# Two layers of Fourier mixing and an MLP on one core: who normalizes the first two pairs of tiles, in which order the first stage makes its parts, and where a weight copy stands

## Chip, cores and metric

The kernel runs on one core of a Trainium2 chip. The metric is the device time of one execution in microseconds (us), from the start of the program to its end; the time of a kernel is the median of its runs. The profile is taken in an execution of its own, and its span runs from the first to the last of the program's instructions.

## The reference, cut to what matters

```python
def layernorm(x, eps=1e-5):
    return (x - mean(x, -1)) / sqrt(var(x, -1) + eps)

def A(x, Cr, Ci, Dr, Di):            # x: 1 x 2048 x 576
    a = einsum("bsd,ed->bse", x, Dr)          # hidden DFT, 576 x 576
    b = einsum("bsd,ed->bse", x, Di)
    return einsum("ts,bse->bte", Cr, a) - einsum("ts,bse->bte", Ci, b)   # sequence DFT, 2048 x 2048

def B(x, w1, b1, w2, b2):            # 576 -> 4608 -> 576
    y = layernorm(x)
    h = gelu(einsum("bsd,df->bsf", y, w1) + b1)
    return einsum("bsf,fd->bsd", h, w2) + b2

for layer in range(2):
    x = x + A(layernorm(x), ...)
    x = x + B(layernorm(x), ...)
```

All data is fp32. The DFT matrices are inputs like any other.

## The kernel before, in words

**Products in three passes.** TensorE multiplies in the format fp32r. Each operand is kept as a high part (a copy rounded to fp32r, made by ScalarE) and a low part (the source less the high part, made by VectorE), and each product is three matmuls: high by high, high by low, low by high (`PASSES`). Large products are also cut into 2 x 2 blocks and done in seven block products instead of eight (`ORDER`, `RIGHT`, `LEFT`), which needs sums and differences of blocks as further operands.

**Stages.** For each of the two layers, a `Sequence` computes the sequence DFT of the normalized x (class `Sequence`, method `run`), leaving its two results per tile of 128 rows in DRAM (`uv_mid`). Then two halves follow, each with a `Hidden` stage (the hidden DFT from `uv_mid` with the matrix `dh`, and the second normalization) and the MLP. In layer 0 the sequence stage also splits w1 into its parts in the background and stores them in DRAM (`w1_parts`, generator `weights`, moved on by calls of `pump`); layer 1 finds them made.

**The first stage of `Sequence.run`.** The 16 tiles of x are handled as 8 pairs p, each 128 x 4 x 288. The first `PLAIN` = 2 rows of output tiles (t = 0, 1, called the plain tiles) are computed with the plain eight products while the pairs come in: `first_mms(p)` issues 48 matmuls of 288 columns, 24 for tile 0 in banks 4 to 7, then 24 for tile 1 in banks 0 to 3. They need, of pair p, the high and low part of the matrix block (`high_left` on ScalarE, `low_left` on VectorE, 128 x 1024) and of the normalized x (`high_z` on ScalarE, 128 x 864 and 128 x 288; `low_z` on VectorE, the same shapes). Beside that each pair gives four differences for the later block products: `right_sums` (one instruction of VectorE, two of GpSimd, into the single buffer `t`), `high_sums` (ScalarE) and `low_sums` (VectorE).

The order of this stage is written by hand in the generator `fill` (the loop `for p in range(NP)`, from L406): each engine gets its instructions in the order in which the calls stand there, and works through them strictly in that order. Before the change, one round p issues: statistics of pair p + 1 (`norm_stats`: bn_stats, bn_aggr and an addition on VectorE, then three small GpSimd instructions: power, product, negation), `high_sums(p - 1)`, `high_parts(p + 1)` (`high_left`, the normalization by ScalarE's activation with bias and scale at L244, `high_z`), `low_left(p)`, at p = 7 also `begin_steps`, then `low_sums(p - 1)`, `low_z(p)`, `right_sums(p)`. Layer 1 (`early` is true) has its first pairs prepared during the MLP before it and shares the rounds from p = 2 on.

**The steps.** After the pairs come 14 output tiles of seven block products each, 98 steps (t, i) in the order `ORDER`. A step is 24 matmuls of 288 columns (`mms`). `begin_steps` makes the first operands: two sums on VectorE (`sums(2)`, 128 x 1024 each) and the high part of step 0. In the loop of `run`, step n issues the low part of step n + 2 (`low`, VectorE; the profile shows all subtractions of the helper `sub` as L197, all additions of `add` as L194), the high part of step n + 3 (`high`, ScalarE, L631), its matmuls, then `post`, which takes the product out of its bank (ScalarE at L661 to L667, or VectorE), and two calls of `pump` unless i = 2. At i = 2 the block sums of the next tile are made (`sums`). The blocks of the sequence matrix (`in_cs`, 512 KB each) come through SyncE's queue into six buffers as they come free.

**The weights in the background.** Each two calls of `pump` make one part: a high part (ScalarE, L270 and L271), a low part (VectorE), and a store to `w1_parts` (SyncE, 320 KB). A part is made in one of three buffers in turn, so the high part of number m waits until the store of number m - 3 has landed.

**The queue.** All DMAs here are issued by SyncE (L191), in the order of the calls. `run` copies b1 into the core and `dh` (nine blocks of 288 KB) into the DRAM tensor `dh_mid`, just after the pairs; `dh_mid` is first read in the last output tile of the sequence stage (`Hidden.begin`).

**The plain tiles' results** are copied out of the banks by ScalarE (`first_post(t)`, four copies at L585) into one buffer that is allocated and freed at once, so the copies of tile 1 wait for the store of tile 0; both are issued after the last parts of the first stage. Step 0 of the steps uses bank 4, so it waits for the copies of tile 0.

## Time and profile before

| what | value |
|---|---|
| median of 3 runs | 2724.04 us (2722.75 to 2724.89) |
| the profiled execution | 2726.73 us |
| its span | 2724.9 us |
| TensorE clock granted, mean | 0.997 |
| TensorE busy | 98% |
| VectorE / ScalarE / GpSimd busy | 65% / 40% / 29% |
| DMA | 544.92 MB, mean 200 GB/s |

The profiled execution's span leaves 1.8 us around it to that execution's time. In timeline rows the columns are: start and duration in us, engine, line, operation, output<-input, shapes, count, and in brackets the idle time of the engine before it with what ended that wait. PE is TensorE, PEld its weight loads, DVE VectorE, ACT ScalarE, POOL GpSimd, SP SyncE; "q" stands for an engine's sequencer. A row can merge several instructions that follow each other closely, and a matmul's shown time includes its way through the array, so a busy PE is not a PE at its full rate: rates are read from counts. The window rows give, for a stretch, its length, the busy time and count of each engine, the granted clock, the share of the DMA engines and GB/s.

### The profile page before, as it was taken

The page shows a single profiled execution, that of the slowest core. Times are in us where ns is not written, and L with a number is a line of the kernel's source. Part 1 is how long each engine was busy: PE and PEld are TensorE (multiplying, and loading weights), DVE is VectorE, ACT ScalarE, POOL GpSimd, SP SyncE. Part 2 cuts the span into 40 slices and gives each one's busy share as a digit, 9 for nine tenths or more (in the row PEclk, how much of TensorE's full clock was granted, in tenths as well). Part 3 has the DMA queues.
Part 4 walks back from the last instruction along what each step waited for, and adds up shares of the span by engine and source line. Part 5 has one row for each costly group of instructions (what it writes and reads, how often), then busy time and mean ns, then how long its engine had stood idle before and what let it go on. Part 6 is the DMA issues. An engine that isn't in the chain of part 4 may idle for free.

```text
span 2724.9 us, 45273 instructions
## 1 busy us (share of the span) xinstructions
PE 2667.4 (98%) x17488; PEld 2498.5 (92%) x17488; DVE 1767.8 (65%) x2582; ACT 1098.2 (40%) x1838; POOL 797.0 (29%) x746
## 2 busy tenths in 40 slices
PE   7999999999999999999999999999999999999998
PEld 7999999888888988988899999998999999898988
DVE  8788876777776565556676666466555556555555
ACT  6555554544443343333344333344333324433331
POOL 5232234544434432222240000043222234322222
PEclk9999999999999999999999999999999999999999
DMA  5676775777777456666453333636666673666664
GB/s 202 235 242 233 239 274 173 254 259 281 270 265 278 154 176 194 193 207 211 152 202 141 122 120 119 201 118 200 194 192 196 190 274 104 211 193 194 193 194 149
DMA packets 209287, 544.92 MB, mean 200 GB/s; under 512 B 22048, under 2 KB 56864, under 8 KB 208928
## 3 DMA queue, kind: packets, MB, share of 16 engines
q1 hardware_dynamic: 209072, 542.02, 60.7%
q8 instruction: 139, 2.28, 0.3%
q14 instruction: 76, 0.62, 0.1%
HBM read 429.87 MB, written 114.72 MB: 200 GB/s over the span
## 4 chain that ended last, share of the span: by engine, by line
PE 82%; DVE 6%; issue 4%; DMA 3%; ACT 2%; POOL 2%; SPq 1%; DVEq 0%; ACTq 0%; POOLq 0%
PE bank L204 80%; DVE R L197 3%; DVE A L197 1%; PE bank L836 1%; DVE A L194 1%; DMA w_parts<-R 1%; POOL A L197 1%; DMA A<-in_w 1%; ACT R L631 1%; SPq L191 1%; DVE moments L234 0%; DMA A<-in_c 0%; ACT A L244 0%; POOL R L197 0%; DMA R<-w_parts 0%
## 5 line engine op out<-in xcount | busy, mean ns | idle before, releaser
L204 PE MATMUL bank<-R 128*128 128x288 f32 (+2 forms) x16972 | 2618.6, 315 | 47.0 <-DVE A L194 15.0
L204 PEld LDWEIGHTS bank<-R 128*128 128x128 f32 x16972 | 2444.0, 189 | 213.3 <-DVE A L194 30.0
L194 DVE TENSOR_TENSOR A<-bank,A 128x576 f32<-128x576 f32 (+3 forms) x808 | 567.6, 710 | 542.6 <-PE bank L204 469.1
L197 POOL TENSOR_TENSOR R<-A,R 128x512 fp32r<-128x512 f32 x288 | 382.7, 1341 | 915.7 <-ACT R L1205 889.3
L197 DVE TENSOR_TENSOR R<-A,R 128x1024 fp32r<-128x1024 f32 (+8 forms) x521 | 486.5, 955 | 72.3 <-ACT R L631 35.4
L194 POOL TENSOR_TENSOR A<-A 128x576 f32<-128x576 f32 (+2 forms) x102 | 133.0, 1308 | 557.3 <-ACT A L669 369.4
L1144 ACT ACTIVATE bank<-bank,b1t 128x512 f32<-128x512 f32 (+1 forms) x224 | 144.7, 646 | 370.5 <-DVE bank L194 253.9
L1205 ACT ACTIVATE R<-A 128x512 fp32r<-128x512 f32 x288 | 175.8, 628 | 269.8 <-DVE A L197 114.5
L197 POOL TENSOR_TENSOR A<-A 128x384 f32<-128x384 f32 (+2 forms) x154 | 196.2, 1276 | 271.3 <-DVE R L197 104.0
L194 DVE TENSOR_TENSOR bank<-bank,A 128x512 f32<-128x512 f32 (+1 forms) x228 | 152.5, 671 | 153.5 <-PE bank L204 152.7
L197 DVE TENSOR_TENSOR R<-bank,R 128x512 fp32r<-128x512 f32 x336 | 209.8, 639 | 59.2 <-ACT R L200 49.3
L631 ACT ACTIVATE R<-A 128x1024 fp32r<-128x1024 f32 x196 | 204.4, 1053 | 92.8 <-DVE A L197 70.4
L197 DVE TENSOR_TENSOR A<-A 128x1024 f32<-128x1024 f32 (+3 forms) x132 | 141.0, 1073 | 6.1 <-ACT A L244 2.1
L1171 ACT ACTIVATE A<-bank 128x512 f32<-128x512 f32 (+1 forms) x76 | 43.7, 575 | 240.0 <-PE bank L204 234.8
L1205 ACT ACTIVATE R<-bank 128x512 fp32r<-128x512 f32 x216 | 121.1, 594 | 34.2 <-PE bank L204 34.2
L270 ACT ACTIVATE R<-A 128x256 fp32r<-128x256 f32 x126 | 52.0, 412 | 118.2 <-DMA w_parts<-R 72.7
L197 DVE TENSOR_TENSOR A<-bank,A 128x512 f32<-128x512 f32 x144 | 98.0, 680 | 0.0
L200 ACT ACTIVATE R<-bank 128x512 fp32r<-128x512 f32 (+1 forms) x112 | 50.0, 492 | 88.0 <-PE bank L836 81.9
L244 ACT ACTIVATE A<-A,moments 128x576 f32<-128x576 f32 x64 | 53.7, 862 | 53.1 <-POOL moments L227 28.2
L1144 ACT ACTIVATE A<-bank,b1t 128x512 f32<-128x512 f32 (+1 forms) x76 | 50.6, 665 | 53.8 <-DVE bank L194 53.7
L671 DVE SCALAR_TENSOR_TENSOR A<-A 128x288 f32<-128x288 f32 x28 | 16.0, 572 | 79.4 <-POOL A L194 79.4
L271 ACT ACTIVATE R<-A,power,middle 128x128 fp32r<-128x128 f32 x126 | 60.7, 482 | 0.0
(58 smaller groups left out, 609.2 us busy)
## 6 DMA issues: line engine op xcount, KB each, us to landing
R<-w_parts SPq DMA_DIRECT2D x504, 320.0 KB, 3.4
R<-w_parts SPq DMA_DIRECT2D x189, 576.0 KB, 3.7
A<-in_cs SPq DMA_DIRECT2D x112, 512.0 KB, 4.2
w_parts<-R SPq DMA_DIRECT2D x126, 320.0 KB, 5.1
w_parts<-R SPq DMA_DIRECT2D x63, 576.0 KB, 5.9
uv_mid<-A SPq DMA_DIRECT2D x32, 576.0 KB, 2.8
A<-in_w SPq DMA_DIRECT2D x72, 192.0 KB, 5.2
R<-dh_parts SPq DMA_DIRECT2D x23, 576.0 KB, 10.3
```

The costliest lines, as they stand in the source:

```text
L191: nc.sync.dma_start(dst, src)
L194: engine.tensor_tensor(dst, a, b, op=op)
L197: engine.tensor_tensor(dst, a, b, op=OP.subtract)
L200: nc.scalar.activation(hi, src, AF.Copy)
L204: nc.tensor.matmul(o, a, b, start=start, stop=stop, skip_group_check=True)
L244: nc.scalar.activation(dst, src, AF.Identity, bias=mv[:, 4:5], scale=mv[:, 3:4])
L270: nc.scalar.activation(t[:, 1:4:2], src[:, 0:3:2], AF.Copy)
L271: nc.scalar.activation(t[:, 2], src[:, 1], AF.Identity, bias=power[:, 2:3], scale=middle)
L631: nc.scalar.activation(self.cells[t, i](2, NP, P)[:, 0], self.source(t, i), AF.Copy)
L1144: nc.scalar.activation(dst, src, AF.Gelu_apprx_tanh, bias=bias(f))
L1171: nc.scalar.activation(up, o, AF.Copy)
L1205: nc.scalar.activation(H[q, k](2, TC)[:, 0], src, AF.Copy)
```

## The change

1. **Normalization of pairs 0 and 1 of layer 0** moves from ScalarE to VectorE: two `tensor_scalar` instructions a pair (128 x 576, subtract the mean, multiply by the power), in place. GpSimd's product and negation for these two pairs go.
2. **A new prelude**: VectorE clears `middle`, ScalarE writes `power` from it (its first activation), and TensorE transposes the identity `WARM` = 56 times into an unused corner of bank 3.
3. **Order in `fill`**: in layer 0 `low_left` and `low_z` of pairs 0 and 1 come first in their rounds; from p = 2 on (both layers) `low_z(p)` comes ahead of `low_sums(p - 1)`, and `right_sums(p)` behind it. `begin_steps` moves from the middle of round 7 to behind the loop.
4. **Plain tiles**: `first_post(0)` is issued right behind the matmuls of the last pair, ahead of `begin_steps` and the last sums, and writes into one of the x buffers; tile 1 gets a buffer of its own.
5. **The copies of b1 and dh** leave their place behind the pairs; they are issued in step n = 7, `dh` as one DMA instead of nine.

```diff
+WARM = 56
...
-    def stats_of_pair(src):
+    def stats_of_pair(src, plain=False):
...
         nc.gpsimd.tensor_tensor(mv[:, :, 3], mv[:, :, 2], power[:, 0:2], op=OP.pow)
+        if plain:
+            return mv
         nc.gpsimd.tensor_tensor(mv[:, :, 4], mv[:, :, 0], mv[:, :, 3], op=OP.mult)
...
+                if p < 2 and not self.early:
+                    self.low_left(p)
+                    self.low_z(p)
+                    yield
                 if p + 1 < NP:
                     self.norm_stats(p + 1)
+                if p == 0 and not self.early:
+                    self.right_sums(0)
+                    self.load_some()
                 if p and (p != 1 or not self.early):
                     self.high_sums(p - 1)
...
                 yield
-                if p > 1 or not self.early:
+                if p > 1:
                     self.low_left(p)
                 if p == 3:
                     self.begin_loads()
-                if p == NP - 1:
-                    self.begin_steps()
+                if p > 1:
+                    yield
+                    self.low_z(p)
                 if p and (p not in (1, 3) or not self.early):
                     self.low_sums(p - 1)
-                if p > 1 or not self.early:
+                if p > 1 or p and not self.early:
+                    self.right_sums(p)
                     yield
-                    self.low_parts(p)
-                    yield
+            self.begin_steps()
             self.high_sums(NP - 1)
             self.low(*self.steps[0])
             self.high(*self.steps[1])
...
         def normalize(self, p):
             for h in range(2):
                 at = slice(2 * h, 2 * h + 2)
+                if p < 2 and not self.early:
+                    v, mv = self.x[p][:, at], self.mv[p][:, h]
+                    nc.vector.tensor_scalar(v, v, mv[:, 0:1], mv[:, 3:4], op0=OP.subtract, op1=OP.mult)
+                    continue
                 normalize(self.x[p][:, at], self.x[p][:, at], self.mv[p][:, h])
...
-        def low_parts(self, p):
-            self.low_z(p)
-            self.right_sums(p)
-            if p == 0:
-                self.load_some()
...
+            outs = [next(b for b in self.xs if b.at >= UV_AT + 4 * D)]
+            self.xs.remove(outs[0])
+            self.first_post(0, outs[0])
             for _ in self.pieces:
                 pass
             hidden.reserve()
-            if not self.early:
-                dma(b1t, b1)
-                for k in range(KH):
-                    dma(dhd[k], dh[k])
             steps = self.steps
             self.low(*steps[1])
             self.high(*steps[2])
-            for t in range(PLAIN):
-                self.first_post(t)
+            for t in range(1, PLAIN):
+                outs.append(A.alloc(2 * D))
+                self.first_post(t, outs[t])
...
                 self.post(t, i)
                 if t == NT - 1:
                     hidden.begin(self, ORDER.index(i))
+                if n == 7 and not self.early:
+                    dma(b1t, b1)
+                    dma(dhd, dh)
                 if i != 2:
                     pump()
                     pump()
...
+    nc.vector.memset(middle, 0.0)
+    nc.scalar.activation(power, middle.to_broadcast([P, 4]), AF.Copy)
     make_identity(nc, ident)
+    for n in range(WARM):
+        nc.tensor.transpose(bank[:, 3, 3 * P:], ident, ident)
```

More of the change, by code (lines that the diff above doesn't have):

```diff
@@ L503, in norm_stats @@
             if p not in self.mv:
-                self.mv[p] = stats_of_pair(self.x[p])
+                self.mv[p] = stats_of_pair(self.x[p], p < 2 and not self.early)
         def normalize(self, p):
@@ L578, in first_mms, with first_post @@
             clock[0] += 1
-        def first_post(self, t):
-            out = A.alloc(2 * D)
+        def first_post(self, t, out):
             uv = out(2, 2, DH)
@@ L587, in first_post @@
             dma(uvd[t], out(2 * D))
-            out.free()
         def load_block(self, t, k, block):
@@ L694, in run @@
             self.high(*steps[2])
-            for t in range(PLAIN):
-                self.first_post(t)
+            for t in range(1, PLAIN):
+                outs.append(A.alloc(2 * D))
+                self.first_post(t, outs[t])
+            for out in outs:
+                clock[0] += 1
+                out.free()
             for n, (t, i) in enumerate(steps):
```

## The prediction

> **What bounds the kernel now.** First the page, for the whole.
>
> ```profile
> span 2724.9 us, 45273 instructions
> PE 2667.4 (98%) x17488; PEld 2498.5 (92%) x17488; DVE 1767.8 (65%) x2582; ACT 1098.2 (40%) x1838; POOL 797.0 (29%) x746
> ```
>
> TensorE is the bound nearly everywhere, so an edit is worth what it takes from, or adds to, TensorE's stops and slow stretches. The change touches the two sequence stages alone; there I read the timeline from 0 to 135 us (layer 0) and from 1340 to 1445 us (layer 1), TensorE's rows first, then whoever releases them.
>
> ```profile
> 5.73 0.72 POOL L238 TENSOR_TENSOR moments<-moments,power 128x2 f32<-128x2 f32 x1 [4.18 <-DVE moments L237]
> 7.68 1.28 ACT L513 ACT_TABLE_LOAD   x1 [7.68 <-DMA A<-in_c]
> 9.94 1.61 ACT L244 ACTIVATE A<-A,moments 128x576 f32<-128x576 f32 x2
> 11.58 0.92 ACT L525 ACTIVATE R<-A 128x864 fp32r<-128x864 f32 x1
> 12.53 1.43 DVE L197 TENSOR_TENSOR R<-A,R 128x864 fp32r<-128x864 f32 x2 [1.02 <-ACT R L525]
> 12.55 0.61 PE L204 MATMUL bank<-R 128*128 128x288 f32 x1 [12.55 <-ACT R L525]
> 13.88 0.75 DVE L197 TENSOR_TENSOR A<-A 128x576 f32<-128x576 f32 x1
> 14.55 1.53 DVE L234 BATCH_NORM_STATS2 moments<-A 128x6 f32<-128x288 f32 x4
> 16.46 3.92 DVE L197 TENSOR_TENSOR R<-A,R 128x1024 fp32r<-128x1024 f32 x4
> 22.90 3.94 DVE L197 TENSOR_TENSOR R<-A,R 128x1024 fp32r<-128x1024 f32 x4
> 23.04 1.64 POOL L238 TENSOR_TENSOR moments<-moments,power 128x2 f32<-128x2 f32 x1
> 54.33 1.83 DVE L194 TENSOR_TENSOR A<-A 128x1024 f32<-128x1024 f32 x1
> ```
>
> Front: ScalarE loads its table only when the matrix block has landed, then left part, normalization and high part stand in one line before the first matmul at 12.55; the second waits until 13.65 for VectorE's low part (second row of the next block). Loop: VectorE never rests, and its round lasts 22.90 - 16.46 = 6.44 us. The rate of TensorE:
>
> ```profile
> 20.00:40.00 20.00, 20.00 (x153) 20.00 (x152) 19.81 (x39) 15.29 (x19) 14.93 (x16) 1.00 0.69 243
> 13.65 4.69 PE L204 MATMUL bank<-R 128*128 128x288 f32 x18 [0.49 <-DVE R L197]
> 381.26 1.14 PE L836 MATMUL bank<-ident,A 128*128 128x128 f32 x9
> 489.90:493.20 3.30, 0.37 (x2) 1.00 1.04 370
> 493.50:496.90 3.40, 3.40 (x9) 0.50 0.65 261
> 497.00:500.40 3.40, 3.40 (x16) 1.00 0.63 151
> ```
>
> Warm, 153 matmuls in 20 us are 0.131 us each, a pair's 48 are 6.3 us: just less than VectorE's round. The first 18 take 4.69 us, 0.24 to 0.26 each, half rate. The clock column has no half rate there, but the last three rows show it elsewhere: after 3.3 us nearly without matmuls the grant is 0.50 for 3.4 us, 9 matmuls instead of 16.
>
> ```profile
> 59.71 7.31 PE L204 MATMUL bank<-R 128*128 128x288 f32 x54
> 67.98 1.29 ACT L585 ACTIVATE A<-bank 128x288 f32<-128x288 f32 x4
> 68.42 26.05 PE L204 MATMUL bank<-R 128*128 128x288 f32 x194 [1.40 <-ACT A L585]
> 72.18 1.32 ACT L585 ACTIVATE A<-bank 128x288 f32<-128x288 f32 x4 [2.91 <-DMA uv_mid<-A]
> 80.98 1.22 DVE L194 TENSOR_TENSOR A<-A 128x1024 f32<-128x1024 f32 x1 [3.79 <-DMA A<-in_cs]
> 95.16 25.44 PE L204 MATMUL bank<-R 128*128 128x288 f32 x190 [0.69 <-DVE R L197]
> 99.52 0.86 SPq L191 DMA_DIRECT2D w_parts<-R  x2
> 101.14 0.42 ACT L270 ACTIVATE R<-A 128x256 fp32r<-128x256 f32 x1 [3.71 <-DMA w_parts<-R]
> 104.19 0.42 ACT L270 ACTIVATE R<-A 128x256 fp32r<-128x256 f32 x1 [1.29 <-DMA w_parts<-R]
> 107.08 0.40 ACT L667 ACTIVATE A<-bank 128x288 f32<-128x288 f32 x1
> 120.94 14.31 PE L204 MATMUL bank<-R 128*128 128x288 f32 x106 [0.34 <-ACT A L661]
> ```
>
> Pairs end at 67.0; the steps start at 68.42, behind the copies of plain tile 0. Then ScalarE is held, in its order, by stores of weight parts.
>
> **The change part by part.** All times are of the profiled execution.
>
> *Front, layer 0.* The table load leaves the line (1.28 us), ScalarE's normalization too (1.61). VectorE normalizes pair 0 from 6.5 (the power ends at 6.45). No row shows that instruction: it takes time, so its bounds are nothing and the 0.75 of the 576-column subtraction at 13.88, which reads two tensors where this one reads one; I take 0.7, the nearest row. Pair 0 is then ready at 7.9, before ScalarE's left part (1.0 us between the table load's end at 8.96 and 9.94, now 7.7 to 8.7). High part 8.7 to 9.6, VectorE's left part 8.8 to 10.0, low part to 11.0. TensorE's second matmul goes at 11.0 instead of 13.65: 2.65 us. If the transposes have warmed the clock, pair 0 takes 6.3 us instead of about 9 (2.7 more).
>
> *But VectorE's line decides.* In the new order the statistics of pair 1 (14.55 to 16.46 before, 1.9 with the small instructions) run at 11.2 to 13.2, GpSimd's power behind a VectorE subtraction to 14.6 (it takes 0.72 alone, 1.64 beside one), normalization to 16.0, high part to 17.0, low part to 18.1. Statistics of pair 2 now come after that (18.4 to 20.3), then GpSimd (an estimate of 2.5: the power at 0.72 to 1.64 and two shorter ones), VectorE's left part of pair 2 beside it, ScalarE 1.6 and 0.9, low part (1.0) done at 26.4. From there a round is 6.44 again: pair 6 is ready at 52.3, pair 7, which has no statistics after it but waits for ScalarE's high part, at 57.3. TensorE stands twice on the way and ends pair 7 near 64.9 instead of 67.0. Of 5.3 us won in front, 2.1 are left. Costed at nothing: GpSimd's two differences, which move with `right_sums`, have a round of 6.44 us until `high_sums` reads them; the loads of pairs 4 to 7, which wait for them in SyncE's queue, land a round or more ahead of their statistics; the two GpSimd instructions dropped and the prelude's small ones lie in engines' idle time before 5.7. Without that cover each would add its 0.2 to 0.8.
>
> *End of the pairs, layer 0.* The sums of step 0 (1.83 at 54.33 and one like it) leave the place ahead of pair 7's low part, and now stand ahead of step 0's own low part. The x buffer that `first_post(0)` takes is pair 7's by the allocation, so two of its copies wait for GpSimd's last differences (about 63.1). Copies to 63.8, high part to 64.8, low part on VectorE to 66.0; step 0 runs as if started at 66.15 against 68.5: 2.35 us. Tile 1's copies no longer wait 2.91 us for a store, so the blocks behind it in SyncE's queue leave 3 us sooner, VectorE's 3.79 us wait begins and ends sooner, and 0.7 of the stop at 95.16 goes. Sum **-3.05**; between -1 (VectorE's line 2 us later than worked out) and -4.5 (VectorE without any wait).
>
> *Layer 1* has no new normalization, only the order.
>
> ```profile
> 1408.75 19.48 PE L204 MATMUL bank<-R 128*128 128x288 f32 x144 [0.33 <-DVE R L197]
> 1423.65 1.83 DVE L194 TENSOR_TENSOR A<-A 128x1024 f32<-128x1024 f32 x1
> 1427.38 2.69 DVE L197 TENSOR_TENSOR R<-A,R 128x1152 fp32r<-128x1152 f32 x3 [0.15 <-ACT R L560]
> 1429.76 6.51 PE L204 MATMUL bank<-R 128*128 128x288 f32 x47 [1.53 <-DVE R L197]
> 1437.73 7.44 PE L204 MATMUL bank<-R 128*128 128x288 f32 x54 [1.45 <-ACT A L585]
> ```
>
> With low z ahead of the sums the stops of 0.33 and 1.53 go (the sums of step 0 and a 1.36 us low sum leave VectorE's line ahead of pair 7): pairs 4 to 7 run 4 x 6.3 us from 1408.3 to 1433.5. Step 0's low part is ready at 1433.7, step 1's about 0.5 late: as if started at 1433.95 against 1437.83, **-3.9** (-2.5 to -4.5).
>
> *The copy of dh* was hidden; its cover was an idle queue.
>
> ```profile
> 42.00:46.00 4.00, 4.00 (x33) 4.00 (x32) 3.92 (x6) 2.50 (x5) 3.56 (x4) 1.00 0.92 336
> 50.00:68.00 18.00, 17.02 (x129) 16.79 (x127) 15.88 (x15) 8.83 (x11) 8.79 (x7) 1.00 0.00 1
> 100.00:116.00 16.00, 16.00 (x123) 16.00 (x123) 13.53 (x16) 8.85 (x16) 4.83 (x4) 1.00 0.83 262
> dh_mid<-in_dh SPq DMA_DIRECT2D x9, 288.0 KB, 6.1
> ```
>
> 2592 KB at 336 GB/s are 7.9 us of all DMA engines; afterwards they did nothing from 50 to 68. In step 7 the copy is issued just ahead of the two stores at 99.52, where the engines are 0.83 busy. The high part at 104.19 waits for the first of these stores (it is the buffer of three parts ago) and goes the moment it lands; behind it on ScalarE stand the high part of step 12 and the copy at 107.08 that frees step 12's bank. TensorE has no reserve there: from 95.16 (third matmul of step 8) the 94 matmuls to step 12 end at 95.16 + 94 x 0.131 = 107.5, and that copy ends at 107.48. So TensorE stands **+7.9** (from 0, if the store overtakes the copy, to 7.9 x 16/9 = 14). After that pause the clock is halved until one whole 3.4 us window was busy: 3.4 to 6.8 us at half rate, **+2.3** (1.7 to 3.4). In the slow stretch the others catch up, so the stop at 120.94 goes: -0.5. One DMA or nine makes no difference to the bytes.
>
> The Trainium skill, "DMA: Bandwidth & Descriptors", section "Queues, rings and completion order", says that each DMA engine takes descriptors of a ring in order. By that rule the store cannot overtake the copy and the sum is the one below; were it otherwise, it would be rival A's. The wait of 3.71 us at 101.14 for a store agrees.
>
> *Sum:* -3.05 - 3.9 + 7.9 + 2.3 - 0.5 = +2.75 us. On the profiled execution's 2726.73 that is 2729.5; that execution lies 2.7 above the median of 2724.04, so I predict 2724.04 + 2.75 = 2726.8.
>
> **The rivals.**
>
> *A, the copy costs nothing* (faster). If the queue lets the stores through, or ScalarE has come 8 us ahead by step 7, only -3.05 - 3.9 = -6.95 is left: 2717.1. For it: VectorE and ScalarE start sooner. Against it: the 3.71 us wait, and no reserve at 107.5.
>
> *B, the transposes don't warm the clock.* The 9 transposes in 1.14 us are 0.109 each (the last one's way through the array, 0.27, taken off); at half rate 56 take 12.2 us, from about 1.4 to 13.6, and the first pair starts cold at the time of before. TensorE is then the bound again and ends pair 7 at 66.5; step 0 gets no stop, as if started at 67.0. Layer 0 keeps 0.85 us less: 2727.7. No row shows 3 us of transposes in a stretch, so the profile can't decide. The Trainium skill, "TensorE: Matmul & The Clock Gate", section "Part 4: PE-mode transpose", says that transposes don't count as activity for the clock; by that rule B is what happens.
>
> *C, the copy costs twice* (slower). As one DMA of nine equal blocks it may be dealt to 9 engines of 16: 14 us instead of 7.9, and the total +8.9: 2732.9. It decides as slower once the copy holds the queue for more than 10.6 us. Against it: nine single blocks ran at 336 GB/s with the engines 0.92 busy. The same page of the skill, section "Why a DMA increments its semaphore by 16 and not by 1", lets the outermost size of an access decide how many engines take part; by that rule nine blocks as they stand would give C, and nine blocks merged into one stretch would not.
>
> **How the numbers follow.** Forecast 0.45, A 0.30, B (with the copy's cost) 0.10, C 0.15. The forecast's own range, from the bounds above without A and C, is 2722 to 2731. For 8 in 10 the range must reach A at one end and most of C at the other: 2716 to 2732.5. About 0.2% (5.4 us) is what a measurement of this kernel can tell from no change, so faster means below 2718.6: three quarters of A, 0.23. Slower means above 2729.5: nearly all of C, a fifth of the forecast and of B, 0.24. The rest, 0.53, lies between.
>
> **What would show it.** In the new profile: the table load near 1 us; first matmuls near 11 us, 0.13 apart if warm and 0.24 if not; TensorE's pair 7 starting near 58.6; first_post(0) waiting for GpSimd; the start of layer 1's steps 3.9 us nearer to the end of its pair 3; and near 104 us a stop of TensorE of about 8 us, released by ScalarE behind a `w_parts` store, with the clock at 0.50 after it. Without that stop I am wrong and A holds; if it is 14 us, C holds. If layer 1 shows no gain, the order of low parts and sums was not what held pair 7.

## The result and the profile after

The kernel after takes 2730.06 us (median of 10 runs, 2727.0 to 2733.73) against 2724.42 us (10 runs of the kernel before beside them): ratio 1.0022, 95% interval 1.0014 to 1.0030. The profiled execution took 2731.4 us, 4.67 us more than that of before. The page of the kernel after, its span and the busy time of its engines:

```profile
span 2729.6 us, 45358 instructions
PE 2677.2 (98%) x17544; PEld 2509.3 (92%) x17544; DVE 1773.8 (65%) x2587; ACT 1096.9 (40%) x1835; POOL 784.6 (29%) x742
```

The shares hardly differ; where the time goes is found by laying the matmuls of both traces side by side. Both have 16972 matmuls on the line of the products (L204 before, L205 after), so the k-th of one stands beside the k-th of the other, counted from 0:

| matmul | before, us | after, us | difference |
|---|---|---|---|
| 0, the first | 12.55 | 9.67 | -2.88 |
| 48, first of pair 1 | 22.43 | 17.01 | -5.42 |
| 336, first of pair 7 | 60.51 | 58.66 | -1.85 |
| 386, third of step 0 | 68.79 | 68.02 | -0.77 |
| 590, in step 8 | 96.87 | 97.92 | +1.05 |
| 1100, behind the copy | 164.97 | 176.06 | +11.09 |
| 8390, 96 ahead of layer 1's pairs | 1369.54 | 1380.28 | +10.74 |
| 8870, layer 1, behind the pairs | 1437.73 | 1444.25 | +6.52 |
| 16971, the last | 2716.38 | 2722.60 | +6.22 |

The first stage gives 5.4 us and loses nearly all of it before the steps begin; something takes 1.8 us more in the first steps; the copy takes 10; layer 1 gives back 4.2. Now each place. The timeline of after, front:

```profile
0.72 1.28 ACT L1334 ACT_TABLE_LOAD   x1 [0.72 <-PEq L1398]
1.35 8.56 PE L1337 MATMUL bank<-ident 128*128 128x128 f32 x56 [1.35 <-POOL ident masks.py:199]
6.50 1.07 DVE L522 TENSOR_SCALAR A<-A,moments 128x576 f32<-128x576 f32 x2 [0.92 <-POOL moments L239]
7.16 1.06 ACT L528 ACTIVATE R<-A 128x1024 fp32r<-128x1024 f32 x1 [4.94 <-DMA A<-in_c]
9.67 0.38 PE L205 MATMUL bank<-R 128*128 128x288 f32 x1
10.50 6.90 PE L205 MATMUL bank<-R 128*128 128x288 f32 x48 [0.46 <-DVE R L198]
13.97 2.03 DVE L522 TENSOR_SCALAR A<-A,moments 128x576 f32<-128x576 f32 x2 [0.60 <-POOL moments L239]
18.15 6.48 PE L205 MATMUL bank<-R 128*128 128x288 f32 x47 [0.75 <-DVE R L198]
26.58 3.71 PE L205 MATMUL bank<-R 128*128 128x288 f32 x26 [0.75 <-DVE R L198]
```

TensorE starts early and near its full rate (48 matmuls in 6.90 us, 0.144 each against 0.131), and then stands before pairs 1 and 2 for VectorE, as the working of the prediction had it (18.1 and 26.4).

One thing moves this whole front from execution to execution: the landing of the first matrix block, for which ScalarE's first left part waits (7.16 us in after; before, the table load waits for it, at 7.68; 6.50 in run 2 and 6.27 to 7.27 in the other runs below). From there on the second matmul of pair 2 comes 19.4 to 19.6 us later in after and in all the runs built on it but 8 and 10, which change that part. So times in the first stage are best counted from this landing. By that count the third matmul of step 0 comes at 61.1 us in before and at 60.9 in after: 0.25 of the 0.77 us in the table are the change's, the other 0.52 are the block that landed sooner.

The end of the pairs and the start of the steps, same view:

```profile
58.12 1.17 ACT L569 ACTIVATE R<-A 128x1152 fp32r<-128x1152 f32 x1 [2.46 <-POOL A L198]
59.32 1.36 DVE L198 TENSOR_TENSOR R<-A,R 128x1152 fp32r<-128x1152 f32 x1 [0.92 <-ACT R L569]
61.62 3.40 POOL L198 TENSOR_TENSOR A<-A 128x288 f32<-128x288 f32 x2 [3.53 <-DVE A L198]
65.05 0.71 ACT L593 ACTIVATE A<-bank 128x288 f32<-128x288 f32 x2 [2.75 <-POOL A L198]
65.65 1.06 ACT L638 ACTIVATE R<-A 128x1024 fp32r<-128x1024 f32 x1
66.74 1.23 DVE L198 TENSOR_TENSOR R<-A,R 128x1024 fp32r<-128x1024 f32 x1 [2.38 <-ACT R L638]
66.76 0.53 PE L205 MATMUL bank<-R 128*128 128x288 f32 x2 [1.59 <-ACT R L638]
68.02 28.21 PE L205 MATMUL bank<-R 128*128 128x288 f32 x190 [0.73 <-DVE R L198]
```

Read it as a chain, from the top down: ScalarE waits for GpSimd before pair 6's sums, VectorE for ScalarE, GpSimd starts pair 7's differences late and ends them at 65.02, the third copy of plain tile 0 waits 2.75 us for that, and the high and the low part of step 0 stand behind it. The stretches of after (columns: length, busy time and count of each engine, then the granted clock, the DMA engines' share, GB/s):

```profile
64.00:67.40 3.40, 1.70 (x11) 1.23 (x10) 1.02 (x2) 2.35 (x4) 1.02 (x1) 1.00 0.25 100
67.40:74.20 6.80, 6.18 (x26) 6.18 (x27) 6.73 (x7) 5.00 (x10) 0.00 (x0) 0.50 0.23 91
111.80:122.00 10.20, 4.81 (x20) 4.81 (x21) 4.86 (x6) 5.21 (x10) 1.82 (x2) 0.50 0.59 207
```

The first one is half idle, the clock of the second is 0.50: 26 matmuls in 6.18 us, 0.238 us each. At 0.131 us they would take 3.4, so this costs up to 2.8 us; from matmul 386 to 577, TensorE goes from 0.77 us ahead of before to 2.02 behind it. The third stretch lies around the copy. Its rows, the two queue rows first (the queue's line is L192):

```profile
91.70 17.22 PE L205 MATMUL bank<-R 128*128 128x288 f32 x129
100.46 0.64 SPq L192 DMA_DIRECT2D dh_mid<-in_dh  x1
101.19 0.99 SPq L192 DMA_DIRECT2D w_parts<-R  x2
113.86 0.42 ACT L273 ACTIVATE R<-A 128x256 fp32r<-128x256 f32 x1 [12.42 <-DMA w_parts<-R]
117.19 7.06 PE L205 MATMUL bank<-R 128*128 128x288 f32 x35 [8.27 <-ACT A L674]
```

No stop shows near 95, and one of 8.27 us comes where ScalarE waits 12.42 us for the store issued just behind the copy. In layer 1 the pairs and the steps run through, 380 matmuls without a row's break:

```profile
1399.83 50.47 PE L205 MATMUL bank<-R 128*128 128x288 f32 x380
```

### The profile page after: what moved, and what is told of

It reads as the page before. It is cut to its first block, busy times and chain, and to the rows that moved or that the text cites. A ratio compares the mean times of both kernels' runs of the same rounds, so it can differ in the third digit from the quotient of the medians.

```text
span 2729.6 us, 45358 instructions
## 1 busy us (share of the span) xinstructions
PE 2677.2 (98%) x17544; PEld 2509.3 (92%) x17544; DVE 1773.8 (65%) x2587; ACT 1096.9 (40%) x1835; POOL 784.6 (29%) x742
## 4 chain that ended last, share of the span: by engine, by line
PE 77%; DVE 4%; issue 2%; POOL 1%; ACT 1%; DMA 1%; SPq 0%; DVEq 0%; POOLq 0%; ACTq 0%
PE bank L205 76%; DVE R L198 2%; PE bank L849 1%; DVE A L195 1%; DVE A L198 1%; POOL R L198 0%; DMA R<-w_parts 0%; POOL A L198 0%; PE bank L920 0%; ACT A L247 0%; DVE moments L220 0%; DMA A<-in_w 0%; DVE bank L195 0%; DVE moments L235 0%; ACT R L201 0%
## 5 line engine op out<-in xcount | busy, mean ns | idle before, releaser
L205 PE MATMUL bank<-R 128*128 128x288 f32 (+2 forms) x16972 | 2620.1, 316 | 42.4 <-DVE A L195 15.2
L205 PEld LDWEIGHTS bank<-R 128*128 128x128 f32 x16972 | 2446.6, 189 | 207.7 <-DVE A L195 31.0
```

What stands on the lines that cost most here:

```text
L205: nc.tensor.matmul(o, a, b, start=start, stop=stop, skip_group_check=True)
```

## The experiments

**Theory:** the slowdown is the place of the copy (step 7 has neither an idle queue nor a reserve), and the small gain of layer 0 is due to GpSimd and the block that `first_post(0)` overwrites. **Rivals:** the copy's form costs (one transfer where there were nine); another part of the change costs; the start of the steps is held by VectorE's two sums; the early warm clock, or VectorE's normalization, is what counts in front.

All runs, with the ratio to the kernel before in the same batch. The last two columns are read from the profiled executions: the time from matmul 590 to matmul 1100, which holds the copy where that stands in the steps, and matmul 386 (the third of step 0) counted from the landing of the first matrix block.

| kernel | median us | ratio, 95% interval | 590 to 1100, us | 386 from the landing, us |
|---|---|---|---|---|
| before | 2724.42 | 1 | 68.1 | 61.1 |
| after | 2730.06 | 1.0022, 1.0014 to 1.0030 | 78.1 | 60.9 |
| 1 copies early | 2719.79 | 0.9984, 0.9975 to 0.9993 | 67.5 | 60.9 |
| 2 copies alone | 2733.53 | 1.0035, 1.0023 to 1.0048 | 78.7 | 61.1 |
| 3 nine copies | 2729.59 | 1.0018, 1.0009 to 1.0027 | 78.1 | 61.0 |
| 4 no transposes | 2718.96 | 0.9980, 0.9971 to 0.9989 | 67.8 | 60.8 |
| 5 steps first | 2718.06 | 0.9977, 0.9968 to 0.9986 | 67.4 | 59.0 |
| 6 other buffer | 2719.13 | 0.9979, 0.9969 to 0.9988 | 68.4 | 59.3 |
| 7 steps' sums in the round | 2718.47 | 0.9977, 0.9967 to 0.9987 | 67.6 | 59.8 |
| 8 pair sums first | 2721.98 | 0.9987, 0.9978 to 0.9995 | 67.8 | 62.6 |
| 9 copies spread | 2723.05 | 0.9998, 0.9989 to 1.0007 | 72.4 | 60.9 |
| 10 ScalarE normalizes | 2720.54 | 0.9987, 0.9978 to 0.9995 | 67.6 | 62.7 |
| 11 both | 2717.12 | 0.9975, 0.9965 to 0.9986 | 68.5 | 59.8 |
| 12 other queue | 2723.97 | 1.0007, 0.9998 to 1.0016 | 75.3 | 60.9 |

### The copy: runs 1, 2, 3, 9 and 12

**1.** The copies of b1 and dh go ahead of `first_post(0)`; the rest of the change stays.

```diff
+            if not self.early:
+                dma(b1t, b1)
+                dma(dhd, dh)
             outs = [next(b for b in self.xs if b.at >= UV_AT + 4 * D)]
...
-                if n == 7 and not self.early:
-                    dma(b1t, b1)
-                    dma(dhd, dh)
```

> The kernel after, with the copies of b1 and dh (still one DMA for dh) issued right behind the pairs, ahead of first_post(0), instead of in step 7. Theory (the place): in step 7 the copy stands in SyncE's queue ahead of the stores of weight parts, ScalarE waits for these, TensorE stops for 8.4 us and then runs 10 us at half clock. So here no stop near 117 us, 8 to 12 us less than the kernel after: 2718 to 2722 us, faster than before by 2 to 6 us. Rival (the stop comes from the new order of parts, and the copy only happens to be near): the stop stays, 2727 to 2731 us.

**2.** The kernel before, with the copies alone moved to step 7 as one transfer.

```diff
-                for k in range(KH):
-                    dma(dhd[k], dh[k])
...
+                if n == 7 and not self.early:
+                    dma(b1t, b1)
+                    dma(dhd, dh)
```

> The kernel before, with nothing changed but the copies of b1 and dh (as one DMA), moved into step 7. Theory (the place): a stop of TensorE of about 8 us near step 12 and half clock behind it, 8 to 11 us slower than before: 2732 to 2735 us. Rival (the new order of parts makes the stop): no more than 1 us from before.

**3.** After, with nine copies of 288 KB in step 7.

```diff
-                    dma(dhd, dh)
+                    for k in range(KH):
+                        dma(dhd[k], dh[k])
```

> The kernel after, with dh copied in step 7 by nine DMAs of 288 KB instead of one. Theory (the place): the bytes ahead of the stores are the same, so within 1.5 us of the kernel after, 2729 to 2732 us, with the same stop of 8 to 9 us. Rival (the form: one DMA in long pieces is what blocks the queue): the stop shrinks by half or more, 2720 to 2726 us.

The first turns the slower kernel into a faster one, and the second makes the kernel before slower alone. TensorE's row of run 1, then the rows of ScalarE and TensorE in run 2:

```profile
94.40 45.83 PE L205 MATMUL bank<-R 128*128 128x288 f32 x344 [0.68 <-DVE R L198]
```

```profile
112.02 0.42 ACT L270 ACTIVATE R<-A 128x256 fp32r<-128x256 f32 x1 [10.32 <-DMA w_parts<-R]
115.35 24.92 PE L204 MATMUL bank<-R 128*128 128x288 f32 x168 [8.57 <-ACT A L667]
```

With the copy out of the way there is no break in 344 matmuls; with it the same stop as in after, in a kernel that has nothing else of the change. After and run 1 differ in the place of the copies only, and 1.0022 - 0.9984 is 10.4 us; the traces give 78.1 - 67.5 = 10.6. Nine copies have the same 78.1. So the place costs, and the form does not.

**9.** After, with one copy of 288 KB in each of the steps 7 to 15.

```diff
-                    dma(dhd, dh)
+                if 7 <= n < 7 + KH and not self.early:
+                    dma(dhd[n - 7], dh[n - 7])
```

> After, with the copy cut in nine of 288 KB, one in each of the steps 7 to 15 rather than all in step 7. Theory Q (the burst costs, because each store of a weight part waits in the queue behind all of it, while 24 matmuls of a step are 3.15 us): one copy of 288 KB is 0.86 us of the DMA engines at 336 GB/s, the engines were 0.83 busy, so each step has 0.5 us idle for it; 0.3 us a step are left over, or less where ScalarE has caught up: 0 to 3 us in all and no pause long enough to halve the clock, 2719.8 to 2722.8, and no stop of TensorE over 1.5 us between 95 and 135 us. Rival W (the bytes cost what they cost, wherever they stand beside the steps): nine stops near 0.9 us, 7.9 us in all, 2727.7.

```profile
108.35 10.36 PE L205 MATMUL bank<-R 128*128 128x288 f32 x74 [1.38 <-ACT A L674]
120.10 12.88 PE L205 MATMUL bank<-R 128*128 128x288 f32 x94 [1.40 <-DVE R L198]
133.88 6.39 PE L205 MATMUL bank<-R 128*128 128x288 f32 x46 [0.89 <-ACT A L674]
```

Three stops of TensorE, of 0.9 to 1.4 us, instead of one of 8.27, and no halved clock behind them. 72.4 - 67.5 = 4.9 us remain, 2723.05 in all: just above what theory Q allowed (2722.8; two stops passed 1.5 us counted from start to start), far below rival W. By the ratios run 9 is 3.8 us above run 1. So spread over the steps the bytes still cost between a third and a half of what they cost in one place; hidden they are not.

**12.** After, with the copy of dh issued from ScalarE's queue.

```diff
-                    dma(dhd, dh)
+                    nc.scalar.dma_start(dhd, dh)
```

> After, with the copy of dh still one transfer in step 7 but issued from ScalarE's queue, not SyncE's; nothing else is moved. Theory R (the stores of the weight parts stand behind the copy because they are in one queue with it): the stores share the DMA engines with the copy and land one after the other while it runs. The copy's 7.9 us of engine time are less the idle share (0.17 of some 16 us when it gets half of the engines, 2.7 us), so 5.2 us of work is pushed back, some of it into the lead of the loads: no stop of TensorE over 4 us between 95 and 135 us, and 2722 to 2726. Rival B (the engines are simply full, in whatever queue the copy stands): one stop of 7 to 9 us near 107 us as in after, and 2729 to 2731.

Rows of the timeline (ScalarE's queue, ScalarE, TensorE), then of the view of the DMA queues from 95 to 125 us (packets, MB, share of 16 engines; the copy is in q10):

```profile
95.14 0.63 ACTq L722 DMA_DIRECT2D dh_mid<-in_dh  x1
107.32 0.42 ACT L273 ACTIVATE R<-A 128x256 fp32r<-128x256 f32 x1 [10.35 <-DMA w_parts<-R]
109.12 0.85 PE L205 MATMUL bank<-R 128*128 128x288 f32 x2 [4.88 <-ACT R L638]
```

```profile
q1 hardware_dynamic: 2369, 5.76, 54.6%
q10 hardware_dynamic: 64, 2.65, 25.4%
```

Neither theory is right as it stands. The stop shrinks to 4.88 us, more than R allowed and less than B, and 75.3 - 67.5 = 7.8 us remain. The median lies in R's range, but in its batch the kernel before is 1.6 us faster than in after's; the ratio, 1.0007, makes 2726.3 of 2724.42. A store issued at 95.47 still takes until 107.22 though no copy is ahead of it in its queue, and lands just behind the copy (106.98); in after the two stores land at 113.77 and 114.57, behind the copy at 112.97. The run also changed more than the queue: ScalarE comes to step 7 about 5 us before SyncE does, so the copy was issued at 95.14 instead of 100.46. What it shows is that order within one queue is not the whole cause: the copy takes the engines from a store beside it too. The Trainium skill, "DMA: Bandwidth & Descriptors", section "Queues, rings and completion order", says that an engine takes turns between queues by whole packets; the packets here are 41 KB for the copy (2.65 MB in 64) and 2.4 KB on the other queue, which would give the copy most of each turn. No run separates that from the rest, so the share of queue order stays open.

### The start of the steps: runs 5, 6, 7, 8 and 11

All these start from run 1.

**5.** The sums and the high part of step 0 go ahead of the copies of plain tile 0.

```diff
+            self.begin_steps()
             outs = [next(b for b in self.xs if b.at >= UV_AT + 4 * D)]
...
-            self.begin_steps()
             self.high_sums(NP - 1)
```

> The copies out of step 7 (as in the run with the copies behind the pairs, 2719.79 us), and in addition the sums and the high part of step 0 stand ahead of the copies of plain tile 0 on VectorE and ScalarE, in both layers. Theory G (in layer 0 the steps start late because ScalarE stands 2.75 us in front of the third copy, for GpSimd's last two differences that read the block written there, and step 0's high part stands behind it): step 0 goes about 1.7 us sooner than in the run with the copies early (there the two stops ahead of the steps are 1.87 and 1.02 us), step 1 stands up to 0.9 us for its own high part: in all 0.8 to 1.7 us less, 2718.1 to 2719.0. Rival S (the steps wait for the two sums of step 0 on VectorE): the start of the steps stays where it was, 2719.8, since the sums end where they ended.

**6.** Plain tile 0 is written over pair 4's block in layer 0.

```diff
-            outs = [next(b for b in self.xs if b.at >= UV_AT + 4 * D)]
+            outs = [next(b for b in self.xs if b.at >= UV_AT + 4 * D or b.at == raw.at and not self.early)]
...
-                out.free()
+                if out.at != raw.at or self.early:
+                    out.free()
```

> The copies out of step 7, and in layer 0 the copies of plain tile 0 are written over the block of pair 4, read long before, not over pair 7's. Theory G (GpSimd's last differences hold the copies and with them step 0): the four copies follow each other without the 2.75 us wait, the high part of step 0 starts about 2.5 us sooner, and the steps start about 2 us sooner: 2717.4 to 2718.2 against 2719.79. Rival S (the two sums of step 0 on VectorE end last): the wait on ScalarE goes and the start of the steps moves by less than 0.5 us: 2719.4 to 2719.8.

ScalarE's and TensorE's rows of run 6:

```profile
53.72 18.50 PE L205 MATMUL bank<-R 128*128 128x288 f32 x136
62.12 0.42 ACT L593 ACTIVATE A<-bank 128x288 f32<-128x288 f32 x1 [0.38 <-PE bank L205]
62.91 0.41 ACT L593 ACTIVATE A<-bank 128x288 f32<-128x288 f32 x1 [0.38 <-PE bank L205]
63.22 1.05 ACT L638 ACTIVATE R<-A 128x1024 fp32r<-128x1024 f32 x1
```

The wait for GpSimd is gone, the third copy follows its bank, the high part comes at 63.22 instead of 64.88 (run 1), and both stops ahead of the steps (1.87 and 1.02 us in run 1, from start to start) are gone from TensorE's row. That is theory G's mechanism; in run 5 too the larger stop goes, and matmul 386 comes at 65.93 instead of 67.25. Counted from the landing, it comes 1.9 us sooner in run 5 and 1.6 in run 6 than in run 1 (59.0 and 59.3 against 60.9), where six executions with the order of after lie between 60.8 and 61.0. The times of the two (ratios 0.9977 and 0.9979 against 0.9984) point the same way, but the intervals overlap. Run 6 missed G's 2717.4 to 2718.2: its pairs ended 1.6 us later (matmul 336 at 59.54 against 57.91; 0.55 of that is the landing), behind a halved clock from 26.9 to 30.3 us that run 1's trace does not have.

**7.** The sums of step 0 are back in the last round, ahead of pair 7's low part.

```diff
+                if p == NP - 1:
+                    self.begin_steps()
                 if p > 1:
                     yield
                     self.low_z(p)
...
-            self.begin_steps()
             self.high_sums(NP - 1)
```

> The copies out of step 7, and the two sums of step 0 back in the last pair's round, ahead of that pair's low part, as before the change, in both layers. Theory O (the gain of layer 1, 3.7 us, comes from what stood on VectorE ahead of pair 7's low part): the sums (1.83 us each, one of them on VectorE there) return 1.5 to 2.5 us to layer 1, as a stop of TensorE within pair 7 or ahead of it, and up to 2 us to layer 0: 2721.5 to 2724. Rival E (the gain comes from the end of the pairs, not from that order): 2719.8, within 0.5 us.

**8.** `low_sums(p - 1)` is back ahead of `low_z(p)`.

```diff
+                if p and (p not in (1, 3) or not self.early):
+                    self.low_sums(p - 1)
                 if p > 1:
                     yield
                     self.low_z(p)
-                if p and (p not in (1, 3) or not self.early):
-                    self.low_sums(p - 1)
```

> The copies out of step 7, and in every round the low half of the sum of the pair before stands ahead of the pair's low part again, as before the change. Theory O: the 1.36 us sum is back on VectorE's line ahead of each low part, so layer 1's pairs 4 to 7 get part of their stops back (1.53 us ahead of pair 7's low part before) and layer 0, which runs by VectorE's line, starts its steps no sooner and up to 1.4 us later: 2721 to 2723. Rival E: 2719.8, within 0.5 us.

Run 7's timeline, VectorE and TensorE in layer 0, TensorE in layer 1; then run 8's TensorE in layer 1:

```profile
55.26 1.83 DVE L195 TENSOR_TENSOR A<-A 128x1024 f32<-128x1024 f32 x1
59.87 9.94 PE L205 MATMUL bank<-R 128*128 128x288 f32 x73 [1.40 <-DVE R L198]
1399.74 45.51 PE L205 MATMUL bank<-R 128*128 128x288 f32 x343
```

```profile
1399.74 28.19 PE L205 MATMUL bank<-R 128*128 128x288 f32 x212
1428.10 17.15 PE L205 MATMUL bank<-R 128*128 128x288 f32 x127 [0.17 <-DVE R L198]
```

Theory O falls for run 7: in layer 1 nothing stops, and in layer 0 the sums bring a stop of 1.40 us ahead of pair 7 but take away the wait behind it, so that matmul 386 comes 0.8 us sooner than in run 1 (66.48), 1.1 counted from the landing. For run 8 it holds in layer 0 only, and there in pair 2: VectorE's low part of pair 2 stands behind the low sum of pair 1, which waits 1.23 us for ScalarE, so TensorE stands 3.35 us ahead of the pair's second matmul instead of 0.76, and the clock is halved behind that stop, at 28.9 us. Matmul 386 comes at 69.59, 2.3 us later than in run 1 (1.7 from the landing). In layer 1 there are 0.17 us of idle time. By time run 8 can't be told from run 1 (0.9987 and 0.9984).

The stretch from matmul 8390 to 8870 holds all pairs of layer 1. It takes 68.2 us before, 64.0 after, 63.6 in run 1, and 64.0 in both 7 and 8. Before, TensorE stood 1.53 us ahead of pair 7's second matmul for VectorE, and 1.45 us ahead of the steps for the copies of plain tile 0. The first stop is gone in run 7 and 0.17 us in run 8: either order alone clears it, and they aren't two gains that add up. The second is gone in both runs too, but both keep the copies of tile 0 early; that their place removed it is argued from the rows, and rival E stays open for this part.

**11.** Runs 6 and 7 together: both diffs above, on run 1.

> The copies out of step 7, plain tile 0's copies over pair 4's block in layer 0, and the two sums of step 0 in the last pair's round ahead of its low part, all three. Theory G with what the single runs showed (the wait of 2.75 us for GpSimd gone, and the sums in a place where VectorE waited anyway): VectorE has nothing left between pair 7 and step 0's low part, so the two stops ahead of the steps (1.87 and 1.02 us in the run with the copies early) stay away even where the clock is full, and the steps start near 64.8 us against 65.99 and 67.25: 2717 to 2718. Rival S (one of the two was the whole gain, the other falls in the same idle time): 2718.5 to 2719.1, the steps starting no sooner than in the better of the two single runs (65.9).

```profile
60.32 11.95 PE L205 MATMUL bank<-R 128*128 128x288 f32 x88 [0.23 <-DVE R L198]
```

Pair 7 runs into the steps without a stop, and this has the lowest median of the study, 2717.12, inside theory G's 2717 to 2718; the ratio is 0.9975 (0.9965 to 0.9986). It is faster than both kernels; than runs 1, 5, 6 or 7 it can't be told apart. Matmul 386 (66.94, or 59.8 from the landing) is no sooner than in runs 5 to 7, again behind a halved clock (26.7 to 30.1), so rival S isn't excluded by this trace.

### The front: runs 4 and 10

**4.** Run 1 with `WARM = 0`. **10.** Run 1 with pairs 0 and 1 normalized by ScalarE.

```diff
-WARM = 56
+WARM = 0
```

```diff
-                if p < 2 and not self.early:
-                    v, mv = self.x[p][:, at], self.mv[p][:, h]
-                    nc.vector.tensor_scalar(v, v, mv[:, 0:1], mv[:, 3:4], op0=OP.subtract, op1=OP.mult)
-                    continue
```

> As e1_copy_early, but with WARM = 0, no transposes. Theory (VectorE's line sets the pairs): the first matmuls go at 240 ns until 16 to 20 us, TensorE is the bound again and ends pair 7 1 to 2 us later than in e1_copy_early, so 0 to 2 us slower than it. Rival (the warm clock is worth all of the 2.6 us that pair 0 gains): 2.5 us or more slower than e1_copy_early, 2722 us or more.

> The copies out of step 7 (2719.79 us), and pairs 0 and 1 of layer 0 normalized by ScalarE again, with the table still loaded early and the matmuls that warm the clock still there. Theory V (from pair 1 on VectorE's line sets when TensorE goes, so what VectorE normalizes is paid there): the first matmul is late by about 0.5 to 1 us, but the steps start 0 to 1 us sooner: 2718.8 to 2719.8. Rival F (VectorE's normalization brings the front forward and that stays): the steps start 0.5 to 1.5 us later: 2720.3 to 2721.3.

TensorE in run 4, then one row of run 1:

```profile
8.62 0.61 PE L205 MATMUL bank<-R 128*128 128x288 f32 x1 [8.62 <-ACT R L540]
9.77 14.34 PE L205 MATMUL bank<-R 128*128 128x288 f32 x95 [0.54 <-DVE R L198]
25.84 4.39 PE L205 MATMUL bank<-R 128*128 128x288 f32 x31 [0.76 <-DVE R L198]
```

```profile
25.81 4.37 PE L205 MATMUL bank<-R 128*128 128x288 f32 x31 [0.76 <-DVE R L198]
```

Without the transposes the first matmul is sooner (8.62 against 10.28, since they don't stand ahead of it), the first ones run slowly, and pair 2 begins at the same time: VectorE's line decides, and the warm clock is worth nothing here. By time run 10 leaves its question open: its median lies where rival F had it, but the interval of its ratio overlaps run 1's. Its trace doesn't. The second matmul of pair 2 in run 10:

```profile
28.39 6.86 PE L205 MATMUL bank<-R 128*128 128x288 f32 x38 [0.75 <-DVE R L198]
```

It waits for VectorE as in run 1, 2.6 us later. Of these, 0.8 are the later landing of the matrix block (7.17 against 6.34), and 1.8 are ScalarE's normalization: VectorE waits 1.25 and 2.99 us for the high parts behind it, and the statistics that follow come later. The 1.8 us are still there at the start of the steps (62.7 against 60.9 from the landing). So theory V falls, and F's mechanism is seen. The stretches of halved clock in this trace (11.8 to 15.2 and 28.9 to 32.3 us) don't explain it, since TensorE is the one that waits at pair 2.

## Why the prediction was right, and where not

Forecast and range hold: 2726.8 was predicted, in 2716.0 to 2732.5, with the copy as the term that eats the gains; the measured difference is +5.6 us instead of +2.75. The time is 0.6 us past the 2729.5 from which the prediction called it slower, with a chance of 0.24 against 0.53 for the middle. The terms:

- **Front:** right. The second matmul at 10.50 (11.0 predicted), pair 1's next matmul at 18.15 (18.1), pair 2's at 26.58 (26.4), pair 7 from 58.66 (58.6) to about 65 (64.9). The block that landed 0.5 us sooner than in before helps in this.
- **Start of the steps:** mis-sized, -0.77 at matmul 386 instead of -2.35, and -0.25 counted from the landing. The failing step is "GpSimd's last differences (about 63.1)": they ended at 65.02, no sooner than before (64.97). The term behind it was put at nothing: "GpSimd's two differences, which move with `right_sums`". Through pair 5 they stand beside the statistics; pair 6's have none to stand beside:

```profile
48.43 1.70 POOL L198 TENSOR_TENSOR A<-A 128x288 f32<-128x288 f32 x2 [2.15 <-DVE A L198]
54.86 3.23 POOL L198 TENSOR_TENSOR A<-A 128x288 f32<-128x288 f32 x2 [2.15 <-DVE A L198]
```

  Beside VectorE's low part of pair 7 they take 3.23 us instead of 1.70, and VectorE's two subtractions there take 2.71 us instead of 1.50 a round earlier. So pair 7's low part ends at 58.40 (57.3 in the working), `high_sums(6)` on ScalarE waits 2.46 us for GpSimd and `low_sums(6)` on VectorE 0.92 for that, and pair 7's differences come after it: 1.1 and 0.92 are the 1.9 us between 63.1 and 65.02. The kernel before has the same in its rows, 3.41 and 3.40 us for the last two pairs. Run 6 shows that the wait for these differences, and not VectorE's sums, held step 0; in after itself VectorE waits 2.38 us for step 0's high part.
- **Clock behind the start:** missing in the sum, +2.8. I gave the halved clock to the copy's stop alone. The stops ahead of the steps are short, but together they idle half of one 3.4 us stretch. Run 1 has the same stops and keeps its clock:

```profile
64.00:67.40 3.40, 1.10 (x7) 0.63 (x6) 1.40 (x2) 2.71 (x4) 0.25 (x1) 1.00 0.43 173
67.40:74.20 6.80, 6.61 (x48) 6.38 (x49) 6.77 (x6) 5.51 (x10) 0.00 (x0) 1.00 0.22 86
```

  The clock's stretches lie elsewhere in that execution, so this term comes and goes from run to run: runs 3 and 4, with the same stops, have one halved stretch there, run 12 none.
- **Stop at 95:** gone in after (-0.85 at matmul 578), but by luck, not for the reason given. In run 1 it is there, 0.68 us ahead of 94.40 as before the change (0.69). It is missing only in after and in runs 3 and 4, where the halved clock made TensorE late.
- **Copy:** right in place (from 108.9 us; the working had 107.5), releaser and size: 8.27 us of idle time against 7.9, then 0.50 on the clock and 0.240 us a matmul (20 in 4.81 us); the whole stretch from 590 to 1100 gives +10.0 where 7.9 + 2.3 - 0.5 = 9.7 were predicted. That the order within the queue is the reason is not shown: in run 12 a store of another queue came no sooner than the copy.
- **Layer 1:** right in size, -4.2 between matmuls 8390 and 8870 (-3.9 predicted). For the stop ahead of pair 7, either of the two orders named is enough (runs 7 and 8); what removed the stop ahead of the steps no run separates.
- **Not in the sum:** -0.35 between 1100 and 8390 and about -1.8 from 8870 to the end of the span (4.7 - 6.5). Of the second, 1.55 lie behind the last matmul: the span ends 8.57 us after its start in before, and 7.0 to 7.2 us after it in all the other traces, run 2's among them. That is chance of the one execution, not the change. The rest has no run of its own.

In the profiled executions: 1.05 (at 590) + 10.04 - 0.35 - 4.22 - 1.8 = 4.7 us. The miss against +2.75 is 4.1 us in layer 0 up to step 8, less about 2 of small terms. So the total lies as near to the forecast as it does in part by luck: the -3.05 for layer 0's first stage is not borne out, and in the profiled executions the chance at the end of the span covers a part of that.

**The rivals.** A is wrong: the copy stops TensorE. C is wrong: the copy's stop is 8.27, not 14, and nine copies (run 3) have the same. B is wrong too, in what it says of the clock. The 56 transposes in two stretches of after:

```profile
1.35:5.90 4.55, 4.55 (x22) 4.55 (x23) 1.95 (x7) 0.86 (x2) 0.42 (x5) 1.00 0.82 248
6.00:9.30 3.30, 3.30 (x32) 3.30 (x31) 2.12 (x3) 2.14 (x3) 0.47 (x1) 1.00 1.03 388
```

22 in 4.55 us, 0.207 each, then 32 in 3.30, 0.103 each: their rate doubles at about 5.9 us, 4.6 us after the first, with nothing else on TensorE, and pair 0 then runs at 0.144 us a matmul. In run 4, without them, 14 matmuls take 3.84 us of busy time from 8.6 to 13.0, and only from 13.1 on 27 go in 3.40. The Trainium skill, "TensorE: Matmul & The Clock Gate", section "Part 4: PE-mode transpose", has it that transposes don't count as activity for the clock; here they did, though the trace, which lists them as `MATMUL`, doesn't show in which mode they ran. But B priced that at 0.85 us, and run 4 shows that it is worth nothing that a trace or a time can tell.

## What to carry to other kernels

A copy that is needed much later was free here where nothing behind it in the queue was awaited soon (run 1 issues it at 37.4 us, and the engines are idle from about 50 on); in the busy steps it cost 10.6 us in one place and 4.9 spread over nine steps. When a front is made faster, follow the first engine that becomes late through to the hand-over to the next stage, and look at the last rounds apart from the others: here 5.4 us won were 0.8 at the steps, since GpSimd and VectorE slow each other down in the last two. Before comparing two traces of a front, find what its first wait is for, and count from there. A wait for a buffer can be undone by taking another block that was read long before, before any order is touched.

## What the runs showed of the hardware

- The clock is halved behind a stretch of 3.4 us that is only about half idle, not wholly: TensorE was busy for 1.70 us of 3.40 ahead of 67.4 in after, for 1.67 of 3.41 ahead of 68.43 in run 3, and for 1.10 ahead of 67.70 in run 4. The changes of the clock in one trace lie whole multiples of 3.41 us apart (67.41, 74.24 and 111.78 in after), and where these stretches begin differs from execution to execution. Runs 1 and 12 have the same stops, but the stretches cut them so that the least busy one has 1.92 and 2.15 us, and the clock stays at 1.00. The limit isn't sharp: in run 6 a stretch with 1.91 us, from 23.45 on, was followed by 0.50. A single trace carries such a term by chance: 1.7 us for 3.4 us at half rate while TensorE is busy.
- GpSimd's two differences (128x288 each, fp32) took 1.70 us together beside VectorE's statistics and 3.23 beside its subtractions; these slowed down too, from 1.05 and 0.45 us (864 and 288 columns) to 1.66 and 1.05.
- The first matrix block landed between 6.27 and 7.68 us in the 14 traces, and the first stage moved with it.
- VectorE's normalization (`TENSOR_SCALAR`, 128x576, fp32) took 1.07 us for two in pair 0 (1.4 in the prediction, 0.7 each) and 2.03 for two in pair 1, the two rows of L522 above.
- One transfer of 2592 KB in ScalarE's queue held a 320 KB store of SyncE's queue until 107.2, nearly as long as in the same queue (12.42 and 10.35 us of ScalarE's wait).
